# Separate homes for float64 words and float32 results, with loads asked for further ahead

## Chip, cores and metric

The kernel runs on one core of a Trainium2 chip. The time is the device time of one execution in microseconds; three runs of the kernel before are shown, and their median is the time to compare with. A profile is one further execution, recorded by the hardware profiler.

## What is computed

Chunked attention (chunks of 64 positions, head dimension 64, 8 heads, 8 sequences of 576 positions) gives 4608 tokens of 512 features, and two gated products follow:

```python
out  = softmax(q_c @ k_c.T / 8) @ v_c          # per chunk and head
x    = out.transpose(0, 2, 1, 3).reshape(4608, 512)
x    = ((x @ w_a) * (x @ w_b)) @ w_out         # d_ff 1536
y    = (((x @ w1) * (x @ w2)) @ w3) @ w_out2   # d_ff 1024
```

q, k and v are float32. The seven weight matrices come as float64, and the core reads them as pairs of 32-bit words.

## The kernel before

**Blocks.** The tokens are cut into nine blocks of 512. Blocks 0 and 1 are worked plainly, with 12 feature tiles f of 128 columns each (`plain_step`): twelve matmuls for `pa`, twelve for `pb`, a product, and the product with `w_out` summed in four PSUM banks (`acc`). Blocks 2 to 7 go in three pairs with seven products per feature tile (`strassen_step`, tiles `P`); block 8 is worked alone. Then the second gated product does the same with 8 feature tiles. Every float32 operand is held as a high and a low fp32r part, so each product is three matmuls.

**Attention.** It runs beside this in units of one block and two heads, which the text calls U0 to U7 (blocks 0 and 1) and V0 onward (blocks 2 and 3). A unit loads q and k into a tile `qk` and v into a tile `v` (two buffers each, with places of their own for a few of the first units), turns q and k with matmuls (`t`, line 467), makes scores (`s`), softmax on VectorE and ScalarE (`e`), turns the result (`f`, line 480) and multiplies with v (`x`, line 396).

**Converting weights.** Class `Conv` turns one tile of 128 x 512 float64 numbers into float32. `load` (line 167) takes one tile of 3 x 512 words per partition from a slot: 2 x 512 raw words that a DMA of 512 KB fills (line 173), and 512 words `b` for the result. `s1` works on VectorE and ScalarE in place (lines 179, 182, 185), `s2` on VectorE (line 193) leaves the float32 result in `b`. What becomes of it is a sink: a pair tile `w` in high and low parts, stored to DRAM as `dw` and, in float32, as `d32`; a `wo` tile, stored as `dwo`; or a plain float32 copy in DRAM. These stores are put in a list and issued on GpSimd's queue by `tick` (line 151).

**Pump and slots.** `Pump` keeps the 76 conversion jobs in order: 36 in the first two blocks, 24 in the pair of blocks 6 and 7, 16 in block 8. A slot is a tag of the one SBUF pool. In the first part six tags take turns (Y0, Y1, Y2, xo4, xo5, xo6), later three (Y0 to Y2, then xo1, xo2, G2). Since raw words and result share a tile, the next load into a tag has to wait until the store that reads the result has landed. Loads are asked for so that three jobs are loaded and not done in the first part, and two later.

**Order.** The program's order is written by hand. Each engine works through its own list in order. Pieces of attention and conversion are emitted between matmul groups by `Track`, by a running sum of costs. SyncE's queue (SP) carries nearly all loads: q, k, v, the weights, the conversions. An instruction that waits there holds up every load behind it. Each SP load also waits on one of eight semaphores that are given in turn (DMAHW0 to DMAHW7), so it waits until the load eight places ahead has landed.

Of the kernel before, what the change touches and what calls it, by code (L numbers as in the profile page):

```python
# [9 lines left out]
F32 = mybir.dt.float32  # L10
F32R = mybir.dt.float32r
I32 = mybir.dt.int32
# [5 lines left out]
P = 128  # L18
NT = 512
# [59 lines left out]
def chunk_attention_two_gated_products(  # L79
# [23 lines left out]
    nc = tc.nc  # L103
# [6 lines left out]
    NF = [FA // P, FB // P]  # L110
# [7 lines left out]
    pool = ctx.enter_context(tc.tile_pool(name="pool", bufs=1))  # L118
# [27 lines left out]
    def settle(n):  # L146
        while asks["done"] < n and asks["left"]:
            nc.sync.dma_start(*asks["left"].popleft())  # L148
            asks["done"] += 1

    def tick(every=False, loads=0):
        settle(asks["done"] + loads)
        for s in stores:
            s[0] += 1
        while stores and (every or stores[0][0] > 1):
            _, queue, to, src = stores.popleft()
            queue.dma_start(to, src)  # L157


    class Conv:  # L160
# [3 lines left out]
        def __init__(self, src, name, k=1):  # L164
            self.src, self.k, self.nm = src, k, name

        def load(self, slot, queue=None):
            self.out = slot.pop("out", None)
            t = pool.tile([P, 3 * NT], I32, name=f"cv_{self.nm}", **slot)
            self.b = t[:, 2 * NT :]  # L170
            raw = t[:, : 2 * NT]
            to = raw.rearrange("p (k n) -> p k n", k=self.k) if self.k > 1 else raw
            (queue or nc.sync).dma_start(to, self.src)
            r = raw.rearrange("p (n two) -> p n two", two=2)
            self.lo, self.hi = r[:, :, 0], r[:, :, 1]
# [10 lines left out]

        def s2(self):
            b = self.b
            if self.out:
                self.w = pool.tile([P, NT], F32, tag=self.out, name=f"cw_{self.nm}")  # L190
            else:
                self.w = b.bitcast(F32)
            nc.vector.scalar_tensor_tensor(
                self.w.bitcast(I32), self.hi, 3, b, op0=ALU.logical_shift_left, op1=ALU.bitwise_or
            )

    class Pump:
# [4 lines left out]
        def __init__(self):  # L202
            self.jobs, self.done, self.begun, self.loaded = [], 0, 0, 0
            self.cap, self.ahead, self.last = 0, 2, None

        def add(self, jobs):
            self.jobs.extend(jobs)

        def load(self, slot, queue=None):
            if self.loaded < self.cap:  # L210
                self.jobs[self.loaded][0].load(slot, queue)
                self.loaded += 1

        def begin(self, n):
            while self.begun < min(n, self.loaded):
                self.jobs[self.begun][0].s1()
                self.begun += 1
# [13 lines left out]
            self.done += 1  # L231

        def flush(self):
            last, self.last = self.last, None
            if last:
                last[0]()
                last[1]()
# [790 lines left out]
    def attention_begins(units):  # L1028
        for u in units[:2]:
            u.load1()  # L1030
            u.load2()
# [45 lines left out]
    def fuse(i):  # L1077
        t = w3t.pop(i)
        ps = bank("D", f"wf_{i}")
        for jj in range(NF[1]):  # L1080
            for wp, gp in SEQ:
                nc.tensor.matmul(  # L1082
                    ps,
                    t[:, gp, jj],
                    wo2[jj // 2][:, jj % 2, wp],
                    start=(jj == 0 and (wp, gp) == SEQ[0]),
                    stop=(jj == NF[1] - 1 and (wp, gp) == SEQ[-1]),
                )
        w = pool.tile([P, 2, DM], F32R, tag="qk", name=f"wf_{i}", bufs=2)
        split(w[:, 0], w[:, 1], ps, nc.vector)  # L1090
        store(dwo[1][i], w.bitcast(F32))

    with tc.manual_schedule():
# [3 lines left out]
        pump = Pump()  # L1097
# [8 lines left out]
            for m, w in enumerate((w1, w2)):  # L1106
                pump.add([float32_job(col_conv(w, f, f"1_{f}_{m}"), d32[1][f][:, m])])
        pump.cap = 3 * NF[0]
        slots = {"n": 0}

        def slot(kind):
            slots["n"] += 1
            n = slots["n"]
            if kind == "L":
                return dict(tag=["xo1", "xo2", "G2"][n % 3])
            return dict(tag=["Y0", "Y1", "Y2", "xo4", "xo5", "xo6"][n % kind])

        def conv_piece():
            def emit():
                pump.run()  # L1120
                while pump.loaded < min(pump.cap, pump.done + 3):
                    pump.load(slot(6))

            return (2.4, False, emit)

        def later_conv(n, kind):

            pump.ahead = 1

            def load():  # L1130
                if pump.loaded < min(pump.cap, pump.done + 2):
                    pump.load(slot(kind))

            begin = lambda: pump.begin(pump.done + 1)
            one = [(1.1, False, begin), (0.7, False, pump.run), (0.3, False, load)]
            return one * n
# [16 lines left out]

        U = [First(T, hp, T) for T in range(2) for hp in range(NHP)]
        for i in range(3):
            pump.load(slot(6), nc.scalar)
        for u in U[:NHP]:
            u.load1()
            u.load2()
# [14 lines left out]
        for t in range(NHP + 3):  # L1174
            if 2 <= t < NHP + 2:
                U[t - 2].soft2()
            if t >= 3:
                U[t - 3].apply()
                U[t - 3].put()
            if 1 <= t < NHP + 1:  # L1180
                U[t - 1].scores()
            if t < NHP:
                U[t].turn()
            if 2 <= t < NHP + 2:
                U[t - 2].flip()
            if 1 <= t < NHP + 1:
                U[t - 1].soft1()
            if t in (1, 2):
                U[t + 3].load1()
            if t in (3, 4):  # L1190
                U[t + 1].load2()
            if t in (1, 2, 4, 5, 6):
                pump.run()
            if t < 3:
                pump.load(slot(6), nc.scalar)
            tick(loads=8)
        units = unit_list(1)
        both = attention_pieces(U[NHP:] + units)
# [3 lines left out]
        for n, (T, f) in enumerate(order):  # L1202
            if T == 0:
                conv = Track([conv_piece()] * (1 if f == 0 else 3), 5 if f + 1 < AHEAD else 8)
                if f + 1 == NF[0]:
                    conv = None
# [104 lines left out]
        def between(got):  # L1311


            w3s, sums = [], []
            turns = [(i, c) for i in range(NF[1]) for c in range(2)]
            for n_, ic in enumerate(turns + [None] * 2):
                if n_ >= 2 and n_ % 2 == 0:
                    w3s.append((1.5, True, lambda i=n_ // 2 - 1: fuse(i)))
                if ic:
                    w3s.append((1.0, True, lambda ic=ic: turn_w3(*ic)))  # L1320
            su = [Sums(1, f, dict(tag=f"xo{3 + f % 2}")) for f in range(READY)]
            sums += [(0.1, False, su[0].load), (0.1, False, su[1].load)]
            for f in range(READY):
                sums += su[f].early_pieces()
                if f + 2 < READY:
                    sums.append((0.1, False, su[f + 2].load))
            conv = later_conv(2 * NF[1], "L")
            return merged((0, 1, w3s), (0, 1, conv), (0.5, 1, sums), (0, 0.5, x2_pieces([0, 1], got)))

        PTS = 7  # L1330
# [3 lines left out]
        j, places = 0, plain[0]  # L1334
        for ph, sb in [(0, sb) for sb in range(1, NSB + 1)] + [(1, sb) for sb in range(NSB + 1)]:
# [5 lines left out]
            if lone:  # L1341
                x, pieces = lone_pieces(x32, f"{ph}{sb}")
                pieces = pieces + o2_pieces()
                pump.cap = len(pump.jobs)
                slots["n"] = -1
                pieces += [(0.1, False, lambda: pump.load(slot("L")))] * 2
            elif not begins:
                x, pieces = strassen_pieces(x32, f"{ph}{sb}", sb == NSB)
            if ph == 0 and sb == 1:
# [5 lines left out]
                pieces = pieces + first_sums[0].pieces()  # L1355
            steps, at, conv = NF[ph], [], []
            if ph == 0 and not lone:
                units = unit_list(sb + 1)
                attention_begins(units)
                if sb == 1:  # L1360
                    settle(units[0].qk_end)
                    load_part(ph, 1, 3)
                work = attention_pieces(units)
                n_pts = PTS * steps + steps - 4
                if sb == NSB - 1:
                    pump.cap += 3 * NF[1]
                    pump.load(slot(3))
                    pump.load(slot(3))
                    conv = later_conv(3 * NF[1], 3)
                    work = merged((0, 1, work), (0, 1, conv))  # L1370
                    n_pts = PTS * steps
                at.append(Track(work, n_pts - 3))
            if not begins:
                burst(ph, j + 1, places, pieces, [] if conv else at, state.pop("ready", None))
            if lone:
# [16 lines left out]
                class After:  # L1392
                    n = 0
# [19 lines left out]
            j, places = block_steps(ph, sb, x, at)  # L1413
# [51 lines left out]
```

## Time and profile before

| What | Value |
|---|---|
| runs | 1654.66, 1654.49, 1661.31 us, median 1654.66 us |
| profiled execution | 1660.61 us, of which the span from first to last instruction is 1658.8 us |
| TensorE (PE) matmuls busy | 95% of the span |
| VectorE (DVE), ScalarE (ACT), GpSimd (POOL) busy | 51%, 33%, 30% |
| mean granted TensorE clock | 0.984 of full |
| DMA | 400.37 MB, mean 241 GB/s |

Busy shares are means over stages that differ. The first 120 us have a PE that is busy six to eight tenths of the time, and after that nine tenths or more. So the rows to read are single gaps of PE and what ended them, and the rows of the SP queue, on which the loads behind those gaps were issued.

### The profile page before, as it was taken

The numbers are of one execution on the slowest core, as the hardware profiler recorded it, in microseconds if no ns is written. First come the engines' busy times: TensorE is split into PE (matmuls) and PEld (weight loads), VectorE is DVE, ScalarE is ACT, GpSimd is POOL, SyncE is SP. The second block draws the span as 40 slices with busy tenths as digits, with TensorE's granted clock in tenths as the row PEclk, the third lists the DMA queues.
The fourth block names the chain that finished last, engine by engine and source line by source line (L and its number), as shares of the span: only waits on it lengthen the run. The fifth ranks groups of instructions, "written<-read, shape, count | busy, mean of one in ns | idle before, by whom it ended". The sixth has DMA issues, their size and how long they took to land.

```text
span 1658.8 us, 24429 instructions
## 1 busy us (share of the span) xinstructions
PE 1568.2 (95%) x8968; PEld 1256.4 (76%) x8968; DVE 852.7 (51%) x1384; ACT 551.8 (33%) x989; POOL 489.7 (30%) x502
## 2 busy tenths in 40 slices
PE   5789999899999999899999899999999999999998
PEld 4568777677776777677777677788878878878887
DVE  5657755777865455645676234544452352342331
ACT  5544444332242222332234222333332332331322
POOL 1213333222252111432224211223432331331432
PEclk8889999999999999999999999999999999999999
DMA  8768876878777777788986888886776676666684
GB/s 222 225 197 268 254 234 190 255 243 240 229 222 212 213 219 211 214 232 299 321 299 216 295 308 303 311 289 247 249 236 213 218 237 211 223 227 200 219 292 160
DMA packets 289975, 400.37 MB, mean 241 GB/s; under 512 B 175680, under 2 KB 196160, under 8 KB 289856
## 3 DMA queue, kind: packets, MB, share of 16 engines
q1 hardware_dynamic: 262688, 309.67, 61.3%
q0 software_dynamic: 23616, 81.80, 12.8%
q10 hardware_dynamic: 3552, 7.34, 1.2%
q8 instruction: 71, 1.16, 0.3%
q14 instruction: 48, 0.39, 0.1%
HBM read 312.74 MB, written 85.98 MB: 240 GB/s over the span
## 4 chain that ended last, share of the span: by engine, by line
PE 75%; DMA 7%; DVE 6%; issue 4%; ACT 3%; SPq 2%; POOL 2%; POOLq 0%; ACTq 0%; DVEq 0%
PE P L829 38%; PE acc L858 19%; PE pa L815 4%; PE pb L815 4%; PE wf L1082 3%; SPq L148 2%; PE pb0L L815 2%; PE pa0L L815 2%; DMA wo<-dwo 2%; PE x L396 1%; DMA cv_w<-in_moe_w_dram 1%; DVE xP L243 1%; DMA qk<-in_q_dram 1%; DMA cv_o<-in_moe_w_out_dram 1%; DVE c L917 1%
## 5 line engine op out<-in xcount | busy, mean ns | idle before, releaser
L829 PE MATMUL P<-xP,w 128*128 128x512 f32 (+1 forms) x3102 | 715.3, 383 | 19.9 <-DVE c L917 12.5
L829 PEld LDWEIGHTS P<-xP,w 128*128 128x128 f32 x3102 | 557.2, 188 | 147.2 <-DVE c L917 18.0
L917 DVE TENSOR_TENSOR c<-P,c 128x512 f32<-128x512 f32 (+1 forms) x228 | 150.5, 662 | 333.2 <-PE P L829 332.2
L914 ACT COPY c<-P 128x512 f32<-128x512 f32 (+1 forms) x228 | 128.6, 564 | 226.4 <-PE P L829 226.1
L945 POOL TENSOR_TENSOR G<-c,c 128x512 f32<-128x512 f32 x68 | 89.4, 1315 | 337.9 <-DVE c L917 337.8
L242 ACT CAST gh<-c 128x512 fp32r<-128x512 f32 x68 | 42.3, 622 | 329.7 <-DVE c L944 329.7
L243 POOL TENSOR_TENSOR gl<-c,gh 128x512 fp32r<-128x512 f32 x68 | 90.2, 1327 | 177.4 <-ACT gh L242 177.4
L858 PE MATMUL acc<-gh,wo 128*128 128x512 f32 x384 | 139.1, 400 | 0.0
L944 DVE TENSOR_TENSOR c<-P,c 128x512 f32<-128x512 f32 x68 | 47.0, 691 | 136.0 <-PE P L829 136.0
L858 PE MATMUL acc<-wo,gh 128*128 128x512 f32 x320 | 111.2, 391 | 0.5 <-ACT gh L242 0.5
L858 PEld LDWEIGHTS acc<-gh,wo 128*128 128x128 f32 x384 | 72.9, 190 | 16.6
L243 DVE TENSOR_TENSOR xP<-xP,xP 128x512 fp32r<-128x512 f32 (+1 forms) x56 | 64.2, 1187 | 25.3 <-ACT xP L242 25.2
L815 PE MATMUL pa<-xq,w 128*128 128x512 f32 x288 | 76.1, 416 | 0.0
L858 PE MATMUL acc<-gl,wo 128*128 128x512 f32 x192 | 75.6, 394 | 0.0
L157 POOL DMA_DIRECT2D dw<-w x58 | 32.5, 560 | 133.0 <-DVE w L243 79.2
L815 PE MATMUL pb<-xq,w 128*128 128x512 f32 x288 | 71.1, 396 | 0.0
L858 PEld LDWEIGHTS acc<-wo,gh 128*128 128x128 f32 x320 | 60.1, 188 | 13.9 <-ACT gh L242 1.0
L815 PEld LDWEIGHTS pa<-xq,w 128*128 128x128 f32 x288 | 57.1, 201 | 13.1
L867 ACT COPY ev<-acc 128x512 f32<-128x512 f32 x72 | 42.4, 589 | 71.8 <-PE acc L858 67.0
L858 PE MATMUL acc<-wo,gl 128*128 128x512 f32 x160 | 63.0, 394 | 0.8 <-POOL gl L243 0.8
L815 PEld LDWEIGHTS pb<-xq,w 128*128 128x128 f32 x288 | 53.0, 188 | 10.9
L1082 PE MATMUL wf<-wo,w3t 128*128 128x512 f32 x192 | 50.2, 421 | 4.8 <-DVE w3t L243 4.6
(154 smaller groups left out, 2327.2 us busy)
## 6 DMA issues: line engine op xcount, KB each, us to landing
w<-dw SPq DMA_DIRECT2D x213, 512.0 KB, 4.3
wo<-dwo SPq DMA_DIRECT2D x168, 512.0 KB, 4.5
dw<-w POOLq DMA_DIRECT2D x58, 512.0 KB, 4.8
w<-dw SPq DMA_DIRECT2D x87, 256.0 KB, 3.4
d<-cv POOLq DMA_DIRECT2D x40, 256.0 KB, 4.7
su<-d SPq DMA_DIRECT2D x20, 512.0 KB, 5.5
cv_o<-in_moe_w_out_dram SPq DMA_DIRECT2D x18, 512.0 KB, 5.8
x2d<-ev POOLq DMA_DIRECT2D x36, 256.0 KB, 4.8
```

The source lines that it names most:

```text
L148: nc.sync.dma_start(*asks["left"].popleft())
L242: nc.scalar.copy(dst_h, src)
L243: eng_l.tensor_tensor(dst_l, src, dst_h, op=ALU.subtract)
L815: nc.tensor.matmul(ps, w[m][:, kk // 2, wp, kk % 2], xq[kk // 2][:, kk % 2, xp], start=(n == 0), stop=(n == 3 * KM - 1),)
L829: nc.tensor.matmul(ps, w[:, wp, kt], x[:, kt, xp], start=(begins and n == 0), stop=(n == 5), skip_group_check=True,)
L858: nc.tensor.matmul(acc[m], a, b, start=(f == 0 and (wp, gp) == SEQ[0]), stop=(f == NF[ph] - 1 and (wp, gp) == SEQ[-1]),)
L867: nc.scalar.copy(t, acc[m])
L914: nc.scalar.copy(t, src)
L917: add = lambda o, a, b: nc.vector.tensor_tensor(o, a, b, op=ALU.add)
L944: nc.vector.tensor_tensor(g, last, c11, op=ALU.mult)
L945: nc.gpsimd.tensor_tensor(g_place(ph, nm.split("_")[0], f, gplaces), c22, c12, op=ALU.mult)
L1082: nc.tensor.matmul(ps, t[:, gp, jj], wo2[jj // 2][:, jj % 2, wp], start=(jj == 0 and (wp, gp) == SEQ[0]), stop=(jj == NF[1] - 1 and (wp, g ...
```

## The change

Raw words and results get homes of their own. `homes` names tags for raw words and tags for results; a tag of 4 x 512 words holds two raw homes or four result homes. In the first part there are eight of each (raw in Y0, Y1, xo4, xo5; results in Y2, xo6), later four of each. The homes are taken in turn and are not allocated anew. Loads are asked for until five jobs are loaded and not done (before three), later three (before two), and three instead of two loads are put ahead of the work in the later parts. `flush` now calls `tick(True)` first, so that waiting stores are issued before the last job's low part.

```diff
-        def load(self, slot, queue=None):
-            self.out = slot.pop("out", None)
-            t = pool.tile([P, 3 * NT], I32, name=f"cv_{self.nm}", **slot)
-            self.b = t[:, 2 * NT :]
-            raw = t[:, : 2 * NT]
+        def load(self, raw, b, queue=None):
+            self.b = b
...
+        def homes(self, raws, bs):
+            self.raw_tags, self.b_tags = raws, bs
+            self.raws, self.bs, self.n = [], [], 0
+
+        def home(self, places, tags, k, size):
+            per = 4 * NT // size
+            n = k % (per * len(tags))
+            if len(places) <= n:
+                t = pool.tile([P, 4 * NT], I32, tag=tags[n // per], name=f"cv{self.loaded}_{tags[n // per]}")
+                places.extend(t[:, i * size : (i + 1) * size] for i in range(per))
+            return places[n]
...
-        def load(self, slot, queue=None):
+        def load(self, queue=None):
             if self.loaded < self.cap:
-                self.jobs[self.loaded][0].load(slot, queue)
+                raw = self.home(self.raws, self.raw_tags, self.n, 2 * NT)
+                b = self.home(self.bs, self.b_tags, self.n, NT)
+                self.jobs[self.loaded][0].load(raw, b, queue)
                 self.loaded += 1
+                self.n += 1
...
         def flush(self):
+            tick(True)
             last, self.last = self.last, None
...
+        pump.homes(["Y0", "Y1", "xo4", "xo5"], ["Y2", "xo6"])
...
-                while pump.loaded < min(pump.cap, pump.done + 3):
-                    pump.load(slot(6))
+                while pump.loaded < min(pump.cap, pump.done + 5):
+                    pump.load()
...
-                if pump.loaded < min(pump.cap, pump.done + 2):
-                    pump.load(slot(kind))
+                if pump.loaded < min(pump.cap, pump.done + 3):
+                    pump.load()
...
-                slots["n"] = -1
-                pieces += [(0.1, False, lambda: pump.load(slot("L")))] * 2
+                pump.homes(["xo1", "xo2"], ["G2"])
+                pieces += [(0.1, False, lambda: pump.load())] * 3
...
-                    pump.load(slot(3))
-                    pump.load(slot(3))
-                    conv = later_conv(3 * NF[1], 3)
+                    pump.homes(["Y0", "Y1"], ["Y2"])
+                    for _ in range(3):
+                        pump.load()
+                    conv = later_conv(3 * NF[1])
```

The order of instructions on PE, DVE and ACT stays as it was. On POOL the low part of each `wo` tile moves behind two stores. On SP the loads move. First place: the SP queue after block 0's attention loads, where the first conversions of the main loop are asked for. `cv` are conversion loads, `qk1_2` the q and k of unit U6, and behind each row stands what it waits for (DMAHW a landed load, DMASW a landed store). Before:

```order
L173 DMA cv_0_2_0_682<-in_moe_w_a_dram 128x4x256 [waits DMAHW2_49,DMASW1_49,DVE_49]
L173 DMA cv_0_2_1_684<-in_moe_w_b_dram 128x4x256 [waits DMAHW3_49,DMASW3_49,DVE_49]
L173 DMA cv_o2_686<-in_moe_w_out_dram 128x1024 [waits DMAHW4_49,Pool_49]
L148 DMA qk1_2_702<-in_q_dram 16x4x64 [waits DMAHW5_49,PE_49]
L148 DMA qk1_2_702<-in_q_dram 16x4x64 [waits DMAHW6_49]
L148 DMA qk1_2_702<-in_q_dram 112x4x64 [waits DMAHW7_49]
L148 DMA qk1_2_702<-in_q_dram 112x4x64 [waits DMAHW0_49]
L173 DMA cv_0_3_0_829<-in_moe_w_a_dram 128x4x256 [waits DMAHW1_49,DMASW6_49,DVE_49]
L148 DMA qk1_2_702<-in_k_dram 16x4x64 [waits DMAHW2_49]
L148 DMA qk1_2_702<-in_k_dram 16x4x64 [waits DMAHW3_49]
L148 DMA qk1_2_702<-in_k_dram 112x4x64 [waits DMAHW4_49]
L173 DMA cv_0_3_1_888<-in_moe_w_b_dram 128x4x256 [waits DMAHW5_49,DMASW0_49,DVE_49]
```

The same place now:

```order
L170 DMA cv6_xo5_681<-in_moe_w_a_dram 128x4x256 [waits DMAHW2_49]
L170 DMA cv6_xo5_681<-in_moe_w_b_dram 128x4x256 [waits DMAHW3_49]
L170 DMA cv0_Y0_250<-in_moe_w_out_dram 128x1024 [waits DMAHW4_49,DVE_49]
L170 DMA cv0_Y0_250<-in_moe_w_a_dram 128x4x256 [waits DMAHW5_49,DVE_49]
L170 DMA cv2_Y1_254<-in_moe_w_b_dram 128x4x256 [waits DMAHW6_49,DVE_49,Activation_49]
L148 DMA qk1_2_701<-in_q_dram 16x4x64 [waits DMAHW7_49,PE_49]
L148 DMA qk1_2_701<-in_q_dram 16x4x64 [waits DMAHW0_49]
L148 DMA qk1_2_701<-in_q_dram 112x4x64 [waits DMAHW1_49]
L148 DMA qk1_2_701<-in_q_dram 112x4x64 [waits DMAHW2_49]
L170 DMA cv2_Y1_254<-in_moe_w_out_dram 128x1024 [waits DMAHW3_49,DVE_49,Activation_49]
L148 DMA qk1_2_701<-in_k_dram 16x4x64 [waits DMAHW4_49]
L148 DMA qk1_2_701<-in_k_dram 16x4x64 [waits DMAHW5_49]
```

The waits on stores (DMASW) are gone from the conversion loads, five of them stand in a row where three stood, and a sixth stands between q and k.

Second place: SP at the start of the pair of blocks 6 and 7. `wo0_2` and `wo0_3` are the weights of the third and fourth of the `acc` groups that PE works next, `qk8_0` the first unit of block 8. Before:

```order
L715 DMA w0_1_3_7034<-dw0_1_1_69 128x512
L173 DMA cv_o2_0_7049<-in_moe2_w_out_dram 128x1024
L173 DMA cv_o2_1_7051<-in_moe2_w_out_dram 128x1024
L701 DMA wo0_2_7057<-dwo0_2_166 128x1024
L148 DMA qk8_0_7045<-in_q_dram 32x16x32 x4
L148 DMA qk8_0_7045<-in_k_dram 32x16x32 x4
L701 DMA wo0_3_7117<-dwo0_3_167 128x1024
```

The same place now:

```order
L726 DMA w0_1_3_7004<-dw0_1_1_69 128x512
L170 DMA cv36_Y0_7019<-in_moe2_w_out_dram 128x1024 x2
L170 DMA cv38_Y1_7023<-in_moe2_w_out_dram 128x1024
L712 DMA wo0_2_7029<-dwo0_2_166 128x1024
L148 DMA qk8_0_7015<-in_q_dram 32x16x32 x4
L148 DMA qk8_0_7015<-in_k_dram 32x16x32 x4
L712 DMA wo0_3_7089<-dwo0_3_167 128x1024
```

A third conversion load of 512 KB stands ahead of `wo0_2` and `wo0_3`.

Third place: SP in block 8, where the loads `su1_0` and `su1_1` (float32 pairs from which VectorE forms sums) stand behind two conversion loads. Before:

```order
L173 DMA cv_1_4_0_9517<-in_moe2_w1_dram 128x4x256 [waits DMASW1_49,DMAHW3_49,DVE_49,Activation_49]
L1228 DMA x2_1_3_9525<-x2d_1_3_215 128x512 [waits DMAHW4_49]
L173 DMA cv_1_4_1_9561<-in_moe2_w2_dram 128x4x256 [waits DMASW2_49,DMAHW5_49,DVE_49,Activation_49]
L735 DMA su1_0_9563<-d32_1_0_156 128x1024 [waits DMAHW6_49]
L735 DMA su1_1_9565<-d32_1_1_157 128x1024 [waits DMAHW7_49]
```

The same place now:

```order
L170 DMA cv60_xo1_8964<-in_moe2_w2_dram 128x4x256 [waits DMAHW4_49,DVE_49,Activation_49]
L1232 DMA x2_1_3_9469<-x2d_1_3_215 128x512 [waits DMAHW5_49]
L170 DMA cv62_xo2_8968<-in_moe2_w1_dram 128x4x256 [waits DMAHW6_49,DVE_49,Activation_49]
L746 DMA su1_0_9506<-d32_1_0_156 128x1024 [waits DMAHW7_49,DMASW5_49,DMASW4_49]
L746 DMA su1_1_9508<-d32_1_1_157 128x1024 [waits DMAHW0_49,DMASW7_49,DMASW6_49]
```

The conversion loads wait for no store any more; the `su` loads now name the stores that wrote what they read.

## Rows read from the trace of the kernel before

**Rows 1.** The page: busy us (share), instructions by engine; ScalarE's evictions (mean ns, idle)

```profile
PE 1568.2 (95%) x8968; PEld 1256.4 (76%) x8968; DVE 852.7 (51%) x1384; ACT 551.8 (33%) x989; POOL 489.7 (30%) x502
...
L914 ACT COPY c<-P 128x512 f32<-128x512 f32 (+1 forms) x228 | 128.6, 564 | 226.4 <-PE P L829 226.1
```

**Rows 2.** Stretches: PE, PEld, DVE, ACT, POOL busy, clock, DMA share, GB/s

```profile
50.00:55.00 5.00, 2.34 (x44) 1.90 (x41) 1.75 (x4) 3.08 (x4) 0.62 (x1) 0.88 1.06 307
80.00:100.00 20.00, 12.67 (x141) 9.20 (x141) 8.88 (x18) 8.15 (x13) 4.26 (x7) 0.87 0.86 255
```

**Rows 3.** SP's waits, first 300 us: us in total, times, longest

```profile
SPq L173 <- DMA d<-cv: 59.4, 15, 13.0
```

**Rows 4.** SP's timeline near 60 us: start, us, instruction

```profile
50.73 3.75 SPq L148 DMA_DIRECT2D qk<-in_k_dram  x3
63.68 0.37 SPq L173 DMA_DIRECT2D cv<-in_moe_w_b_dram  x1
64.09 0.59 SPq L148 DMA_DIRECT2D qk<-in_k_dram  x1
```

**Rows 5.** PE's timeline, 60 to 112 us: start, us, instruction [idle before <-releaser]

```profile
68.19 1.09 PE L467 MATMUL t<-ident,qk 128*128 128x128 f32 x4 [4.32 <-DMA qk<-in_k_dram]
...
70.53 1.12 PE L480 MATMUL f<-ident,e 128*128 128x128 f32 x4
...
81.86 0.63 PE L467 MATMUL t<-ident,qk 128*128 128x128 f32 x4 [1.91 <-DMA qk<-in_k_dram]
...
94.80 1.09 PE L467 MATMUL t<-ident,qk 128*128 128x128 f32 x4 [2.21 <-DMA qk<-in_k_dram]
97.09 1.12 PE L480 MATMUL f<-ident,e 128*128 128x128 f32 x4 [1.20 <-ACT kT L468]
...
99.94 5.36 PE L815 MATMUL pa<-xq,w 128*128 128x512 f32 x12
...
108.61 3.03 PE L815 MATMUL pa<-xq,w 128*128 128x512 f32 x12
```

**Rows 6.** DVE's timeline: the softmax results of U5 and U7

```profile
67.90 0.69 DVE L370 TENSOR_TENSOR e<-e,sm 128x512 f32<-128x512 f32 x1
...
94.12 0.69 DVE L370 TENSOR_TENSOR e<-e,sm 128x512 f32<-128x512 f32 x1
```

**Rows 7.** All conversion loads of the tile cv: issue to landing

```profile
DMA to landing us min/median/max: 2.8/4.7/9.5
```

**Rows 8.** DVE's timeline, 740 to 800 us: conversions that waited for their load

```profile
741.85 0.43 DVE L179 TENSOR_SCALAR cv_o<-cv_o 128x512 int32<-128x512 uint32 x1 [3.06 <-DMA cv_o<-in_moe_w_out_dram]
...
751.71 0.43 DVE L179 TENSOR_SCALAR cv_o<-cv_o 128x512 int32<-128x512 uint32 x1 [5.47 <-DMA cv_o<-in_moe_w_out_dram]
...
798.56 0.43 DVE L179 TENSOR_SCALAR cv_w<-cv_w 128x512 int32<-128x512 uint32 x1 [4.57 <-DMA cv_w<-in_moe_w_dram]
```

**Rows 9.** PE's timeline, 700 to 803 us: its long gaps

```profile
700.57 0.47 PE L858 MATMUL acc<-gh_5b,wo 128*128 128x512 f32 x1 [3.48 <-DMA wo<-dwo]
...
744.22 4.46 PE L829 MATMUL P<-xP,w 128*128 128x512 f32 x18 [2.08 <-ACT c L914]
...
754.12 2.93 PE L829 MATMUL P<-xP,w 128*128 128x512 f32 x6 [3.36 <-DVE c L917]
...
800.37 2.81 PE L829 MATMUL P<-xP,w 128*128 128x512 f32 x11 [1.58 <-DVE c L944]
```

**Rows 10.** SP's timeline, block 8

```profile
990.17 0.49 SPq L1228 DMA_DIRECT2D x<-x2d  x1
997.39 0.38 SPq L173 DMA_DIRECT2D cv<-in_moe_w_dram  x1
997.82 0.98 SPq L735 DMA_DIRECT2D su<-d  x2
```

**Rows 11.** DVE's timeline, block 8

```profile
1004.37 0.43 DVE L743 TENSOR_TENSOR su<-su 128x256 f32<-128x256 f32 x1 [2.61 <-DMA su<-d]
```

**Rows 12.** PE's timeline, block 8

```profile
990.57 5.79 PE L1082 MATMUL wf<-wo,w3t 128*128 128x512 f32 x24
...
1008.50 7.38 PE L1082 MATMUL wf<-wo,w3t 128*128 128x512 f32 x24 [2.23 <-DVE w3t L243]
```

More of the change, by code (lines that the diff above doesn't have):

```diff
@@ L188, in s2 @@
             b = self.b
[L189 to L192, printed above, removed]
+            self.w = b.bitcast(F32)
             nc.vector.scalar_tensor_tensor(
@@ L204, in __init__ @@
             self.cap, self.ahead, self.last = 0, 2, None
+            self.raws, self.bs, self.n = [], [], 0
+        def homes(self, raws, bs):
+            self.raw_tags, self.b_tags = raws, bs
+            self.raws, self.bs, self.n = [], [], 0
+        def home(self, places, tags, k, size):
[5 more added lines that the diff above has]
+            return places[n]
         def add(self, jobs):
             self.jobs.extend(jobs)
-        def load(self, slot, queue=None):
+        def load(self, queue=None):
             if self.loaded < self.cap:
-                self.jobs[self.loaded][0].load(slot, queue)
+                raw = self.home(self.raws, self.raw_tags, self.n, 2 * NT)
+                b = self.home(self.bs, self.b_tags, self.n, NT)
+                self.jobs[self.loaded][0].load(raw, b, queue)
                 self.loaded += 1
+                self.n += 1
         def begin(self, n):
@@ L1120, in emit, with later_conv @@
                 pump.run()
-                while pump.loaded < min(pump.cap, pump.done + 3):
-                    pump.load(slot(6))
+                while pump.loaded < min(pump.cap, pump.done + 5):
+                    pump.load()
             return (2.4, False, emit)
-        def later_conv(n, kind):
+        def later_conv(n):
             pump.ahead = 1
             def load():
-                if pump.loaded < min(pump.cap, pump.done + 2):
-                    pump.load(slot(kind))
+                if pump.loaded < min(pump.cap, pump.done + 3):
+                    pump.load()
             begin = lambda: pump.begin(pump.done + 1)
@@ L1155, in chunk_attention_two_gated_products @@
         for i in range(3):
-            pump.load(slot(6), nc.scalar)
+            pump.load(nc.scalar)
         for u in U[:NHP]:
@@ L1194, in chunk_attention_two_gated_products @@
             if t < 3:
-                pump.load(slot(6), nc.scalar)
+                pump.load(nc.scalar)
             tick(loads=8)
@@ L1326, in between @@
                     sums.append((0.1, False, su[f + 2].load))
-            conv = later_conv(2 * NF[1], "L")
+            conv = later_conv(2 * NF[1])
             return merged((0, 1, w3s), (0, 1, conv), (0.5, 1, sums), (0, 0.5, x2_pieces([0, 1], got)))
```

7 lines of the change are left out of this document (removed).

## The prediction

> **What bounds the kernel now.** I read the page's busy shares first: TensorE (PE) is busy 95% of the span [rows 1], so the change can pay only where PE stands idle or runs at the lower clock. The stretches show where: from 80 to 100 us PE is busy 12.67 of 20 us at a mean clock of 0.87 [rows 2]. Then SP's waits: in the first 300 us its queue stood 59.4 us at the conversion loads of line 173, fifteen times, until a store of an earlier result had landed [rows 3]. The timeline of SP shows who pays. Three of the four k loads of unit U6 were out at 54.48 (50.73 + 3.75), then a conversion load stood until 63.68, and the fourth k load went out at 64.09 [rows 4]. PE waited 4.32 us for it, and 1.91 and 2.21 us for the k of U7 and V0, whose loads stood in the same queue [rows 5]. The reader should see one pattern three times: a load that PE needs behind a load that waits for a store.
>
> From about 105 us on PE is nearly full until the later conversions. There VectorE (DVE) itself waits for conversion loads, and PE gaps follow at once; and in block 8 SP stands again. These are terms 2 and 3.
>
> **Term 1, blocks 0 and 1.** The DMASW waits go from the conversion loads, so SP no longer stands there. The raw home they take was read by VectorE eight jobs before. I follow PE's chain. U6's k in time takes away 4.32 us, but the next link, U5's `f`, needs the softmax result that DVE ends at 67.90 + 0.69 = 68.59 [rows 6], and nothing in that DVE work waits for a load. `f` ran at 70.53 [rows 5], so 1.9 us are gained and DVE is late next. U7's k: 1.91 more, together 3.8. V0's k: 2.21 more, 6.0. U7's `f`, at 97.09, needs `e`, ended at 94.81 [rows 6]; moved by 3.8 that is 91.0, and 97.09 - 6.0 = 91.1, so the 6.0 hold. The `pa` behind it took 5.36 us at the lower of the clock's two levels (1.2 GHz), against 3.03 for the next one at 2.4 [rows 5]: if PE does not run dry before it, 2.3 us more. The gap before it shrinks but does not vanish, so I count half, 1.2.
>
> Against this stands traffic. From 50 to 55 us the DMA engines were full (share 1.06, 307 GB/s [rows 2]). Two more conversion loads of 512 KB now stand ahead of U6's k, which is 1.05 MB / 307 GB/s = 3.4 us. So the last k goes out at about 54.5 + 0.6 + 3.4 = 58.5 and lands 4.7 to 9.5 us later (median and longest of such loads [rows 7]), at 63.2 to 68.0; `f` of U5 loses nothing while k lands before about 67. U7 and V0 have less slack, and I take 2.2 off for them. Term 1: 6.0 + 1.2 - 2.2 = 5.0 saved, with bounds at 8.3 (no lateness, full clock) and at a loss of 15 (rival D).
>
> The Trainium skill (DMA: Bandwidth & Descriptors, "Queues, rings and completion order") says that a DMA engine takes a queue's descriptors in ring order, which speaks against long loads ahead of short ones. The spread from 2.8 to 9.5 us [rows 7] agrees with it, though no row separates the order from the load. By that rule alone, five loads ahead of U6's q put it off by an estimated 2.6 MB at 307 GB/s, 8.5 us, and the slack above would be nearly used up; the 2.2 us stand for that here.
>
> **Term 2, blocks 6 and 7.** Three conversions waited for their load, 3.06, 5.47 and 4.57 us [rows 8], and PE gaps of 2.08, 3.36 and 1.58 us start right there [rows 9]: DVE and ScalarE hold PSUM evictions behind the waiting conversion. Each load now stands one job earlier, and the first of the three goes out before the stretch. A job takes several us here, so the waits of DVE should go. I count 1.5 of the first gap (an eviction by ScalarE, 564 ns [rows 1], is late next) and the other two whole: 6.4. Behind the 3.36 us gap six matmuls took 2.93 us where eighteen had taken 4.46 (six: 1.5), so 1.4 for the clock, 7.8 in all. What it costs: a third load ahead of `wo0_3`, for which PE already waited 3.48 us at 700.57 [rows 9]: 0.52 MB / 307 GB/s = 1.7 us longer, and half of another 1.4 us for a clock that may fall in that gap. Net 5.4 saved; bounds 8.4 saved and 3.1 lost.
>
> **Term 3, block 8.** SP stood from 990.66 to 997.39 at a conversion load, and the `su` loads behind it went out at 997.82 [rows 10]. DVE waited 2.61 us for them [rows 11], PE 2.23, and the 24 matmuls after the gap took 7.38 us against 5.79 in an earlier group [rows 12]. With up to 6.7 us in hand the wait goes: 2.23 + 1.6 = 3.8 saved. The bounds are 3.8 and nothing; I take the upper, since 6.7 is far more than 2.61.
>
> **The rest I cost at nothing.** The wait for a store now stands on DVE (line 179 of the changed kernel), before it writes a result home. Behind it in DVE's list stand PSUM evictions that PE needs. But it is the store of eight jobs ago, later four, and each store is issued by the next job or two; if that cover fails, each such wait is a PE gap like the three of term 2. On POOL a `wo` low part goes behind two store issues, and is not needed before a later step. The other SP waits in the first part lie beside a busy PE.
>
> Sum: 5.0 + 5.4 + 3.8 = 14.2 us, 1660.61 - 14.2 = 1646.4 on the profiled execution. That execution lies 5.95 us over the median of 1654.66. If this excess sits in the stalls that go, 1646.4 is the answer against the median also; if not, it is 1640.5. I take the middle, 1643.
>
> **Rivals.**
>
> B: the DMA is the bound at the start. q and k come late as before, behind more conversion loads, and term 1 is nil; the full engines at 50 to 55 us speak for it, the 63.2 to 68.0 us against it. 1643 + 5 = 1648.
>
> C: other engines take over in blocks 6 to 8. PE then waits for evictions or `w3t` instead of conversions, and terms 2 and 3 give nothing. For: in two of the three places it is an eviction that PE names. Against: these follow the DVE wait within 1.5 us. 1643 + 5.4 + 3.8 = 1652.
>
> D, slower: eight loads in flight. Each SP load waits for the load eight places ahead to land, so at the median 4.7 us a load costs 0.59 us of queue, as much as its issue (0.59 [rows 4]). If landings rise, the queue slows by an eighth of the rise per load. From U6's first k to V0's last k stand about 35 loads. At a mean of 4.7 + 8 x 6.0 / 35 = 6.1 us the gain of 6.0 is gone; at the longest landing, 9.5 us [rows 7], it is 35 x 4.8 / 8 = 21 us, a loss of 15. The same would hold up blocks 6 and 7, so term 2 goes too: 1643 + 5 + 15 + 5.4 = 1668. For it: 1.06 of DMA share. Against: from 80 to 100 us the share is 0.86, and only two loads are added once, not at each job.
>
> E: the change doesn't do what it says. SP stands as long as before, at the q and k buffers or the v buffers instead of the stores, which come free only as PE goes on. Then 1654.7.
>
> **How the numbers follow.** Forecast 0.60 (1636 to 1649), B 0.15, C 0.11, D 0.07, E 0.07. What a measurement of this kernel can tell from no change is about 0.5%, 8 us: below 1646.4 is faster, above 1662.9 slower. The forecast gives 0.54 of its 0.60 to faster, B 0.06 and C 0.02: 0.62 faster; D 0.07 slower; 0.31 the same. A range from 1635 to 1654 holds the forecast, B and C, and leaves out D and E with most of the rest, under 2 in 10.
>
> **What would show it.** Right: no wait of SP at the conversion loads for stores; the gaps of PE before U7's and V0's `t` gone or under 0.5 us, and `f` of U5 waiting for DVE's `e` instead; the three DVE waits of blocks 6 and 7 and the one for `su` gone; the gap before `wo0_3` longer by 1 to 2 us. Wrong: landings of q and k beyond 6 us in the first 100 us; DVE waits at the result homes; PE gaps in blocks 6 to 8 of the same sum under other names.

## The result, and the profile after

| | before | changed |
|---|---|---|
| runs, median (lowest to highest) | 1654.86 (1654.49 to 1661.31) us | 1638.49 (1637.16 to 1640.50) us |
| profiled execution, span | 1660.61, 1658.8 us | 1640.50, 1638.7 us |

The ratio is 0.9889, with a 95% interval of 0.9868 to 0.9910: 1.1% faster. Forecast were 1643 us, range 1635 to 1654.

**Blocks 0 and 1.** SP's waits in the first 300 us of the changed kernel (total us, times, longest) answer to [rows 3]; behind them PE's own wait for the softmax result, over the whole span:

```profile
SPq L148 <- PE x L407: 51.6, 9, 13.1
...
SPq L170 <- DVE cv_xo L187: 2.4, 3, 1.9
```

```profile
PE f L491 <- DVE e L381: 12.2, 7, 3.2
```

The wait for stores is gone. SP stands nearly as long as before, but at v loads whose buffers PE has yet to free. No q or k that PE needs is held up behind them: SP's timeline and PE's show it. SP's timeline, against [rows 4]:

```profile
52.04 1.72 SPq L170 DMA_DIRECT2D cv_Y<-in_moe_w_out_dram  x1
53.81 4.41 SPq L148 DMA_DIRECT2D qk<-in_k_dram  x3
58.49 0.38 SPq L170 DMA_DIRECT2D cv_xo<-in_moe_w_a_dram  x1
58.98 0.58 SPq L148 DMA_DIRECT2D qk<-in_k_dram  x1
```

U6's last k goes out at 58.98 (58.5 was forecast, 64.09 before) and lands 6.5 us later, at 65.48. PE's timeline, against [rows 5], and then DVE's softmax results of U5 and U7, against [rows 6]:

```profile
65.68 0.63 PE L478 MATMUL t<-ident,qk 128*128 128x128 f32 x4 [1.12 <-DVE cv_Y L179]
...
69.44 1.09 PE L491 MATMUL f<-ident,e 128*128 128x128 f32 x4 [2.44 <-DVE e L381]
...
78.16 1.04 PE L478 MATMUL t<-ident,qk 128*128 128x128 f32 x8
...
88.65 1.06 PE L478 MATMUL t<-ident,qk 128*128 128x128 f32 x8 [0.26 <-PE acc L869]
...
91.63 0.63 PE L491 MATMUL f<-ident,e 128*128 128x128 f32 x4 [1.92 <-DVE e L381]
...
94.00 5.31 PE L826 MATMUL pa<-xq,w 128*128 128x512 f32 x12
...
102.63 3.03 PE L826 MATMUL pa<-xq,w 128*128 128x512 f32 x12
```

```profile
68.60 0.69 DVE L381 TENSOR_TENSOR e<-e,sm 128x512 f32<-128x512 f32 x1
...
90.80 0.69 DVE L381 TENSOR_TENSOR e<-e,sm 128x512 f32<-128x512 f32 x1
```

The `t` of U7 and V0 wait for nothing that matters, and what is late next is `e`: 68.60 + 0.69 = 69.29, and `f` starts at 69.44. The 1.12 us before U6's second `t` at 65.68 are put down to VectorE, but the last k landed only 0.2 us before it. `f` would have waited for `e` all the same. The `pa` behind U7's `f` still takes 5.31 us where the next takes 3.03. The DMA engines stay full near 50 us, and the clock of the stretch from 80 us is no better than in [rows 2], though PE is busy 16.00 of its 20 us there instead of 12.67:

```profile
50.00:55.00 5.00, 2.01 (x22) 1.59 (x26) 2.32 (x6) 3.08 (x4) 2.22 (x3) 0.96 1.11 361
80.00:100.00 20.00, 16.00 (x149) 12.04 (x148) 10.93 (x21) 8.49 (x16) 3.15 (x4) 0.83 0.77 216
```

**Blocks 6 and 7.** Of the three DVE waits of [rows 8] one of 0.77 us is left (745.53). PE's timeline, against [rows 9]:

```profile
692.94 0.76 PE L869 MATMUL acc<-gh_5b,wo 128*128 128x512 f32 x1 [4.42 <-DMA wo<-dwo]
...
749.43 3.06 PE L840 MATMUL P<-xP,w 128*128 128x512 f32 x12 [0.53 <-ACT c L925]
...
752.91 1.67 PE L840 MATMUL P<-xP,w 128*128 128x512 f32 x6 [0.42 <-ACT c L925]
```

The gap at `wo` grew from 3.48 to 4.42 us, and the matmul behind it now takes 0.76 us instead of 0.47: the lower level of the clock. Two further traces of before have gaps of 4.27 and 3.39 us there, both followed by that lower level (their lines stand with those traces below), so most of this difference is one between executions. Instead of 2.08, 3.36 and 1.58 us, PE loses 0.53 and 0.42, to ScalarE's evictions.

**Block 8.** SP's timeline, against [rows 10]; DVE's start on `su`, against [rows 11]; PE's group at the place of the gap, against [rows 12]:

```profile
974.94 0.41 SPq L170 DMA_DIRECT2D cv_xo<-in_moe_w_dram  x1
975.45 1.14 SPq L746 DMA_DIRECT2D su<-d  x2
```

```profile
986.07 0.41 DVE L754 TENSOR_TENSOR su<-su 128x256 f32<-128x256 f32 x1
```

```profile
990.67 5.85 PE L1093 MATMUL wf<-wo,w3t 128*128 128x512 f32 x24
```

No wait is left there; 24 matmuls take 5.85 us instead of 7.38. The `su` loads went out that much earlier but also landed more slowly, 9.6 and 10.4 us after their issue instead of 6.5 and 7.3.

**The ledger.** Both kernels issue the same 8,968 matmuls in the same order. So the start of each can be set against its twin, and the growth of the difference tells in which stretch (times of before) the 20.13 us from trace to trace were gained:

| stretch, us | gained | forecast |
|---|---|---|
| 0 to 500 (term 1) | 6.2 | 5.0 |
| 500 to 530 | 2.5 | 0 |
| 530 to 690 | 0.3 | 0 |
| 690 to 730 (the gap at `wo`) | -3.4 | -2.4 |
| 730 to 810 (term 2) | 8.7 | 7.8 |
| 810 to 990 | 1.2 | 0 |
| 990 to 1030 (term 3) | 3.8 | 3.8 |
| 1030 to the end | 0.8 | 0 |

### The profile page after: what moved, and what is told of

It reads as the page before. It is cut to its first block, busy times and chain, and to the rows that moved or that the text cites. A ratio compares the mean times of both kernels' runs of the same rounds, so it can differ in the third digit from the quotient of the medians.

```text
span 1638.7 us, 24412 instructions
## 1 busy us (share of the span) xinstructions
PE 1561.4 (95%) x8968; PEld 1253.9 (77%) x8968; DVE 854.8 (52%) x1384; ACT 550.5 (34%) x989; POOL 489.9 (30%) x502
## 4 chain that ended last, share of the span: by engine, by line
PE 77%; DVE 7%; DMA 5%; issue 4%; ACT 3%; POOL 2%; SPq 1%; POOLq 0%; DVEq 0%; ACTq 0%
PE P L840 40%; PE acc L869 19%; PE pa L826 4%; PE pb L826 4%; PE wf L1093 3%; DMA wo<-dwo 3%; PE pb0L L826 2%; PE pa0L L826 2%; PE x L407 1%; SPq L148 1%; DVE xP L254 1%; DMA qk<-in_q_dram 1%; DVE c L928 1%; PE s L356 1%; ACT xP L253 1%
## 5 line engine op out<-in xcount | busy, mean ns | idle before, releaser
L869 PEld LDWEIGHTS acc<-wo,gh 128*128 128x128 f32 x320 | 60.1, 188 | 13.4 <-ACT gh L253 1.0
L373 ACT ACTIVATE e<-e 128x512 f32<-128x512 f32 x36 | 22.8, 633 | 94.2 <-DVE e L367 94.2
```

The source lines that it names most:

```text
L869: nc.tensor.matmul(acc[m], a, b, start=(f == 0 and (wp, gp) == SEQ[0]), stop=(f == NF[ph] - 1 and (wp, gp) == SEQ[-1]),)
```

## The experiments

Ratios are to runs of before on the same chip. The theory: in the first part it is the homes apart that gain, because SP no longer stands for stores; in blocks 6 and 7 it is the third load ahead. The rival: depth is what counts everywhere.

**Three ahead in the first part, homes apart.**

```diff
-                while pump.loaded < min(pump.cap, pump.done + 5):
+                while pump.loaded < min(pump.cap, pump.done + 3):
```

> The changed kernel with its separate homes, but in blocks 0 and 1 loads asked for three jobs ahead again instead of five. Theory S (the early gain comes from SP no longer standing at conversion loads for stores, the depth gives nothing there): TensorE is ahead of the kernel before by 6 us at its 112th us as in the changed kernel, time 1638.5 within 1.5 us. Rival A (the early gain comes from loads asked for further ahead): the 6 us go back, 1644 to 1645.

Measured: 1639.16 us, ratio 0.9899 (0.9877 to 0.9920). Five ahead gives nothing over three. In its trace PE stands at U6's `t` no more, and all of the lateness has become a wait for DVE, about as long as the 1.12 and 2.44 us of the changed kernel together:

```profile
68.91 1.08 PE L491 MATMUL f<-ident,e 128*128 128x128 f32 x4 [3.74 <-DVE e L381]
```

**Five ahead, joint slots.** The kernel before, with only this:

```diff
-                while pump.loaded < min(pump.cap, pump.done + 3):
+                while pump.loaded < min(pump.cap, pump.done + 5):
```

> The kernel before with its joint slots, but loads in blocks 0 and 1 asked for five jobs ahead. Theory S: a load now takes the slot of a job finished two jobs ago, whose store has only just been issued, so SP stands longer at the conversion loads than the 59 us before, q and k come later: 1656 to 1662, slower than 1654.9. Rival A: the depth is what counts, 5 to 6 us are gained, 1649.

Measured: 1720.59 us, ratio 1.0392 (1.0365 to 1.0419). The direction was expected, the size was missed by about 60 us. SP's wait in the first 300 us, then PE's longest gaps:

```profile
SPq L173 <- DMA d<-cv: 135.5, 18, 22.4
```

```profile
77.41 1.08 PE L467 MATMUL t<-ident,qk 128*128 128x128 f32 x4 [7.47 <-DMA qk<-in_k_dram]
101.03 1.09 PE L467 MATMUL t<-ident,qk 128*128 128x128 f32 x4 [13.75 <-DMA qk<-in_q_dram]
...
124.25 1.08 PE L467 MATMUL t<-ident,qk 128*128 128x128 f32 x4 [8.48 <-DMA qk<-in_q_dram]
...
156.59 2.15 PE L467 MATMUL t<-ident,qk 128*128 128x128 f32 x8 [13.54 <-DMA qk<-in_q_dram]
```

With six slots, a load five ahead takes the slot of the last but one finished job, whose store has only just been handed on; three ahead it was a job two places older. Eighteen loads waited for a store, 7.5 us in the mean, where fifteen had waited 4.0 us, and the q and k behind them waited as well. The same depth that is free with homes apart costs 3.9% without. This kernel also lacks the `tick(True)` in `flush`.

**Two ahead from block 6 on, homes apart.**

```diff
-                if pump.loaded < min(pump.cap, pump.done + 3):
+                if pump.loaded < min(pump.cap, pump.done + 2):
```

(and two loads in advance instead of three)

> The changed kernel, but in blocks 6 to 8 loads asked for two jobs ahead again and two instead of three ahead of the work. Theory S with depth as the cause of the gain in blocks 6 and 7: VectorE waits again 3 to 5 us at two or three conversions there and TensorE has its gaps of 2 to 3.4 us back, about 10 us lost, while the 3.2 us that the third load ahead of the wo loads cost come back: 1645. The gap at the su loads of block 8 stays away, since SP waits for no store. Rival: in blocks 6 and 7 too it was SP's wait for stores; then nothing is lost there, the 3.2 us come back, 1635.

Measured: 1646.49 us, ratio 0.9948 (0.9925 to 0.9971). The three DVE waits are back, and PE's gaps with them:

```profile
736.04 0.43 DVE L176 TENSOR_SCALAR cv_Y<-cv_Y 128x512 int32<-128x512 uint32 x1 [2.07 <-DMA cv_Y<-in_moe_w_out_dram]
...
746.57 0.43 DVE L176 TENSOR_SCALAR cv_Y<-cv_Y 128x512 int32<-128x512 uint32 x1 [6.15 <-DMA cv_Y<-in_moe_w_out_dram]
...
794.58 0.43 DVE L176 TENSOR_SCALAR cv_Y<-cv_Y 128x512 int32<-128x512 uint32 x1 [4.43 <-DMA cv_Y<-in_moe_w_dram]
```

```profile
738.41 4.41 PE L840 MATMUL P<-xP,w 128*128 128x512 f32 x18 [1.04 <-ACT c L925]
...
748.98 2.93 PE L840 MATMUL P<-xP,w 128*128 128x512 f32 x6 [4.12 <-DVE c L928]
```

So homes apart alone, with two loads ahead, give blocks 6 and 7 nothing, and the third load gives all of term 2; a third load with joint slots was not run. Block 8 kept its gain. The 3.2 us expected back at `wo` did not come: PE's gap there is 3.39 us, again with the lower clock, and in the ledger below that stretch is about 1 us better than in the changed kernel.

**Without the stores issued at `flush`.**

```diff
         def flush(self):
-            tick(True)
```

> The changed kernel without the new tick(True) in flush, so GpSimd's queue has the low part of each wo tile ahead of the two stores again. Theory S: no load waits for these stores any more, so nothing changes: 1638.5 within 1.5 us. Rival: the earlier stores have a part in the gain, and 2 us or more are lost.

Measured: 1639.33 us, ratio 0.9900 (0.9878 to 0.9922): nothing, as expected, as long as homes are apart. With joint slots it is another matter, as the first part put back will show.

**The three loads of blocks 6 and 7 in the burst.** The burst is the pieces of work with which a pair of blocks begins; the loads go to its end, behind the q and k loads and the first `wo` loads.

```diff
-                    for _ in range(3):
-                        pump.load()
+                    pieces += [(0.1, False, lambda: pump.load())] * 3
```

> The changed kernel, with the three conversion loads of blocks 6 and 7 asked for at the end of block 6's first burst instead of ahead of its q, k and wo loads. My theory (the loads ahead of wo cost what term 2 takes off): the gap of PE before the matmul that waits for wo, 4.42 us in the changed kernel, falls to about 1.5 to 2.5 us, the low clock behind it goes, DVE's conversions still find their data, and the time is 1635 (1633 to 1637). Rival 1: the gap is that of the q and k loads, which stand ahead of the wo load in SP's queue as well; it stays at 3.5 us or more and the time at 1638. Rival 2: the first conversions of blocks 6 and 7 now wait for their loads, and a gap of 2 us or more stands between 725 and 770 us: 1640 or more.

Measured: 1635.55 us, ratio 0.9867 (0.9847 to 0.9887). The gap, then the stretch from 680 us in the changed kernel and in this one (the number before the last two is the granted clock):

```profile
687.84 0.47 PE L869 MATMUL acc<-gh_5b,wo 128*128 128x512 f32 x1 [1.65 <-DMA wo<-dwo]
```

```profile
680.00:720.00 40.00, 33.78 (x136) 26.02 (x135) 22.11 (x23) 15.86 (x29) 16.97 (x15) 0.96 0.86 250
```

```profile
680.00:720.00 40.00, 35.87 (x151) 27.59 (x150) 21.88 (x22) 18.14 (x33) 18.32 (x17) 1.00 0.90 283
```

The gap is 1.65 us and the clock stays up. The loads ahead of `wo` were its cause, and both rivals fall. This moves all three loads, two of which stood ahead of `wo` in the kernel before too.

**The same, with three ahead in the first part** (the first and the last edit together).

> The kernel before this one (loads of blocks 6 and 7 in the burst), and three loads ahead instead of five in the first part. My theory: five ahead gave nothing over three, so this is the same time, 1635 (1633 to 1637), and PE's gap in front of U6's t shorter by about 1 us. Rival: with the later cost gone, the lead of five in the first part shows, and this is slower by 2 us or more.

Measured: 1637.62 us, just above the range, ratio 0.9877 (0.9855 to 0.9899), no different from the one before. PE's gap in front of U6's `t`, 1.29 us there, is gone, but the wait of `f` for `e` grew from 2.25 to 3.75 us.

**The later part alone, and the first part alone.** In the first kernel the first part has six joint slots and three ahead again, in the second the later parts have three joint slots and two ahead. Both keep the `tick(True)` in `flush`. Of the edits, the line that joins the first part's slots:

```diff
-        pump.homes(["Y0", "Y1", "xo4", "xo5"], ["Y2", "xo6"])
+        pump.homes(["Y0", "Y1", "Y2", "xo4", "xo5", "xo6"], [])
```

> The changed kernel with the first part put back: six joint slots and three loads ahead there, homes apart and three ahead from block 6 on. My theory: the two parts add up. SP's wait for stores in the first 300 us is back at about 59 us, with PE's gaps of 4.3, 1.9 and 2.2 us before the t of U6, U7 and V0; the rest of the gain stays: 1645 (1643 to 1648). Rival: a time gained early runs into a later bound, so the early part is worth nothing by the end: 1639.

> The changed kernel with the later parts put back: three joint slots, two loads ahead, two loads in advance from block 6 on; the first part as changed. My theory: term 1 alone is left, 6 us: 1649 (1647 to 1651), and the gap of 2.2 us at w3t in block 8 is back, since there it is the homes apart and not the depth that gained (with homes apart and two ahead it was gone, and the time 1646.5). Rival: the gain in block 8 came from somewhere else in the changed order, the gap doesn't come back, and the time is 1646.5.

Measured: 1641.63 us, ratio 0.9915 (0.9891 to 0.9938), and 1646.71 us, ratio 0.9936 (0.9915 to 0.9957). Both expectations were too slow: the halves gain 0.85% and 0.64%, the whole 1.1%, so they add up only at the edge of their intervals. For the first part alone it is the rival's time and the rival's sign that came. Two things stand out. With the first part put back, SP waited 44.0 us at the conversion loads and not 59.4:

```profile
SPq L170 <- DMA d<-cv_Y: 24.4, 6, 7.4
SPq L170 <- DMA d<-cv_xo: 19.6, 7, 4.2
```

PE's gaps before the `t` of U6, U7 and V0 were 1.23, 1.62 and 0.26 us, not the 4.3, 1.9 and 2.2 expected. The kernel gives a cause: with `tick(True)` in `flush`, GpSimd issues the store behind which U6's fourth k load stands ahead of the `wo` low part. That store in the kernel before, the same in this one, and the conversion load that waited for it (63.68 in [rows 4]):

```profile
58.40 0.55 POOL L157 DMA_DIRECT2D d<-cv  x1
```

```profile
51.27 0.55 POOL L157 DMA_DIRECT2D d<-cv_xo  x1
58.67 0.37 SPq L170 DMA_DIRECT2D cv_xo<-in_moe_w_b_dram  x1
```

It goes out 7 us earlier and lands at 58.6 instead of 63.6. So this kernel is not the first part as it was, and part of term 1 may be there with joint slots: up to 3.6 us by the ledger below, where the third trace of before has 1.9 without the early stores. That is one reason why the halves gain more than the whole. No run has the early stores alone.

And with the later parts put back, the gap in block 8 did not return, though SP stood 4.6 us there (979.91 + 0.50 to 985.01):

```profile
979.47 0.38 SPq L170 DMA_DIRECT2D cv_G<-in_moe_w_dram  x1
979.91 0.50 SPq L1237 DMA_DIRECT2D x<-x2d  x1
985.01 0.38 SPq L170 DMA_DIRECT2D cv_xo<-in_moe_w_dram  x1
985.43 0.98 SPq L751 DMA_DIRECT2D su<-d  x2
```

```profile
990.71 0.43 DVE L759 TENSOR_TENSOR su<-su 128x256 f32<-128x256 f32 x1
```

Here the store goes out no earlier than before: in both kernels GpSimd issues it 15.6 us before PE is done with the matmuls ahead of that place (1006.27 - 990.68 and 995.25 - 979.67). So either the first trace of before was an unlucky one, or the homes are not the cause in block 8. The next two runs ask for it; the expectation takes the earlier landing in the first part for chance as well.

**The kernel before, a second and a third trace.** No edit.

> The kernel before, unchanged, for a second trace of it. With the first part put back and the same order of SP, the store that U6's fourth k load stands behind landed 5 us earlier than in the first trace of before. My theory: the landing of a store differs from execution to execution, and the first trace is a late one; here the load goes out at 58 to 62 us instead of 64.09, PE's gap before U6's t is 1 to 3 us instead of 4.32, block 8's gap at w3t is under 1 us, and the span is 1650 to 1656. Rival: the traces of one kernel agree, the gaps are 4.3 and 2.2 us again, and the difference lies in the kernels.

> The kernel before, unchanged, for a third trace. Theory and rival as for the second: by the theory the span and PE's early gaps go together (a trace that is longer has the larger sum of gaps before 110 us and in block 8).

Measured: 1660.91 and 1660.59 us, spans 1659.1 and 1658.8. PE's first gap, the one at `wo` in block 6 and the one in block 8, second trace, then third (here with the `f` behind the first gap):

```profile
68.02 1.09 PE L467 MATMUL t<-ident,qk 128*128 128x128 f32 x4 [4.29 <-DMA qk<-in_k_dram]
...
699.21 0.77 PE L858 MATMUL acc<-gh_5b,wo 128*128 128x512 f32 x1 [4.27 <-DMA wo<-dwo]
...
1008.89 6.47 PE L1082 MATMUL wf<-wo,w3t 128*128 128x512 f32 x20 [2.09 <-DVE w3t L243]
```

```profile
66.27 0.63 PE L467 MATMUL t<-ident,qk 128*128 128x128 f32 x4 [1.45 <-DMA qk<-in_k_dram]
...
69.69 0.68 PE L480 MATMUL f<-ident,e 128*128 128x128 f32 x4 [2.10 <-DVE e L370]
...
699.36 0.77 PE L858 MATMUL acc<-gh_5b,wo 128*128 128x512 f32 x1 [3.39 <-DMA wo<-dwo]
...
1008.52 6.70 PE L1082 MATMUL wf<-wo,w3t 128*128 128x512 f32 x21 [1.96 <-DVE w3t L243]
```

The theory half falls. The early gap does differ from execution to execution (4.32, 4.29, 1.45 us), but the span does not follow it, and the gap in block 8 is there each time (2.23, 2.09, 1.96). The kernel with five ahead and joint slots has it too (2.09). In the kernel with the first part alone, the first `su` load landed 5.3 us after its issue (985.43) against 6.5 (997.82), and SP went on 5.3 us after GpSimd issued the store that it waited for (979.67 to 985.01) against 6.7 (990.68 to 997.39). Together that is the 2.6 us of [rows 11]. From the store's issue to the landing of `su` it took 11.0 us here, and 13.4 to 13.7 us in the four traces with the gap. No run shows what made them quicker.

**The changed kernel and the one with its loads in the burst, on one chip.**

> The changed kernel, unchanged, on the same chip as the one with its loads in the burst. Ratio to before 0.989 (0.987 to 0.991), and a gap before the matmul that waits for wo in block 6 of 4 us or more, since it came in four traces of kernels with three loads ahead of wo.

> The kernel with the three loads in the burst, a second time, against the changed kernel on one chip. My theory: 3 us below it (1 to 5), from the gap at wo (1.7 us instead of 4.4) and the low clock behind it. Rival: no difference, the two ratios of before came from different chips.

Measured: 1638.86 us, ratio 0.9888 (0.9867 to 0.9908), with a gap of 3.65 us at `wo`, somewhat under the 4 expected; and 1636.47 us, ratio 0.9880 (0.9858 to 0.9903), with its longest gap there 1.10 us. The second is 2.4 us lower, and all three measurements with the loads in the burst (0.9867, 0.9877, 0.9880) lie below the four with homes apart throughout, a third load and the loads in front (0.9888 to 0.9900). The intervals overlap, so about 2 us is likely and not shown. Its traces do show 2.9 us in that stretch (below).

**All traces in one ledger.** Gained against the mean of the three traces of before, by the starts of the matmuls as above, us:

| kernel | 0 to 112 | 500 to 530 | 690 to 730 | 730 to 810 | 990 to 1030 |
|---|---|---|---|---|---|
| before, three traces | -1.0, -0.9, 1.9 | -0.9, 1.7, -0.8 | 1.6, -1.3, -0.3 | 0.9, -1.1, 0.3 | -0.1, 0.0, 0.1 |
| changed, two traces | 5.0, 7.5 | 1.6, 1.7 | -1.8, -1.5 | 9.6, 9.8 | 3.7, 3.6 |
| three ahead; no stores at `flush` | 7.4, 4.7 | 2.0, 1.5 | -0.6, -0.8 | 9.9, 10.6 | 3.6, 3.7 |
| loads in the burst, three traces | 8.0, 4.6, 5.9 | 2.2, 2.4, 2.1 | 1.7, 2.3, 1.0 | 10.5, 10.6, 10.5 | 3.7, 3.6, 3.7 |
| two ahead later | 7.2 | -2.7 | -0.6 | 0.1 | 3.7 |
| first part alone | 6.3 | 1.6 | 0.7 | 2.2 | 3.7 |
| later part alone | 3.6 | 1.6 | -1.1 | 9.5 | 3.6 |
| joint slots, five ahead | -46.8 | 1.4 | 1.2 | 2.0 | 0.0 |

The 2.9 us: 1.7 (mean of 1.7, 2.3, 1.0) against -1.2 (mean of -1.8, -1.5, -0.6, -0.8). In this stretch the traces line up by the loads ahead of `wo`: none, 1.0 to 2.3; two, -1.3 to 1.6; three, -1.8 to -0.6.

## Why the prediction was right

**Term 1, the mechanism right, two parts of the sum wrong.** Every step of the chain is in the trace: U6's last k at 58.98, `f` of U5 waiting for `e`, `t` of U7 and V0 without a wait, U7's `e` ending at 91.49 (91.0 forecast). The first link gave 1.1 us (`f` at 69.44 for 70.53) and not 1.9, since U5's `e` itself ended 0.7 later; by the `pa` behind U7's `f` nearly all of the 6.0 was there (94.00 for 99.94). So the 2.2 us taken off for lateness were hardly due: the loads did land later (in the first 110 us a median of 5.0 to 5.5 us for the two conversion tiles against 4.9, longest 10.1 against 6.5; U6's four q loads 8.1 to 10.2 against 5.7 to 6.7), but what was left in hand covered it. The 1.2 us for the clock did not come: a gap of 1.92 us stood before `f`, and `pa` behind it took 5.31 us. That the two errors nearly cancel, 6.2 for 5.0, is luck. In the third trace of before U6's `t` waits only 1.45 us, and `f` then waits 2.10 us for `e`: that `e` is late next holds without the change too, and part of this term belongs to the one execution from which it was read. That SP's wait for stores was the cost is shown. Which part of the change is needed to take it away is not: homes apart suffice without the deeper loading and, in another run, without the early stores, but the early stores took part of it with joint slots, and homes apart also make eight raw homes out of six slots. More joint slots were not run.

**Term 2, the mechanism right, the gain too small and the loss too large.** 8.7 for 7.8 was gained in the stretch (9.5 to 10.6 against the mean of the three traces of before), since the first gap (2.08 us) went whole where ScalarE's eviction was to be late next. At `wo` 3.4 for 2.4 was lost between the two first traces, but the first trace of before is the best of its three there. Against their mean the five traces with three loads in front lose 0.6 to 1.8 us, and the half of a clock loss in the forecast isn't shown as a cost of the change: two of three traces of before run at the lower level there too. The kernel with its loads in the burst shows that loads in front of `wo` make that gap, and the one with two ahead shows that the gain needs the third load.

**Term 3, the size right, the cause shown with one exception.** With homes apart and two ahead the gap was gone, so depth isn't needed. In all four traces of kernels with joint slots and the old `flush`, SP stood 5.0 to 6.7 us and the gap is there. In the one of the first part alone SP stood 4.6 us and it is not, by the 2.6 us that store and `su` loads landed sooner. So the stand made the gap only together with landings as slow as in those four. The upper bound was the lucky choice: of the 6.7 us in hand the slower landing of `su` took 3.

**What wasn't forecast** is 2.5 us at 512 to 521: PE has a gap at `wo` there in all kernels (1.96 us before, 1.50 after), and from 516 to 525 us the granted clock is 0.81 in two of the three traces of before, and 1.00 in the third and in both of the changed kernel. The trace of before whose clock stayed up has the changed kernel's time there (1.7 in the ledger), and the kernel with two ahead later lost 2.7 there with a clock of 0.57 from 508 to 516 us. So it goes with the clock's level, which no step explains. The other 2.3 us are shifts that no run was made for.

**From the trace to the median.** The sum of 14.2 was 20.1 from trace to trace and 16.4 from median to median. I took half of the 5.95 us by which the profiled execution lay above the median as lying in the stalls that go. The two further traces of before lie as high (1660.91, 1660.59), but runs without the profiler beside them have a median of 1658.04 and reach 1662.80. So whether the excess belongs to profiled executions or to chance stays open, and that the middle came near is luck in part.

**The rivals.** B fell: U7's and V0's q and k came in time, and U6's last k before `e` was done. C fell: the other engines took 0.95 us in blocks 6 and 7. D's landings rose by under 1 us in the median, short of the 6.1 us where it decides. E was half right, which the forecast had at 0.07: SP does stand nearly as long as before, at the v buffers (51.6 us for 59.4), but no gap of PE from 60 to 112 us names a v load.

**The signs.** One sign of being wrong came and proved a poor one: landings of q and k beyond 6 us in the first 100 us. U6's q took up to 10.2 us, but the kernel before already had 6.7, and the gain came all the same. The other two did not: DVE waits for no store at the result homes, and the gaps in blocks 6 and 7 did not come back under other names.

## What to carry over

Where a buffer takes a load and also holds a result until its store has landed, the load queue waits for stores; give raw data and results buffers of their own before asking for more loads ahead, for with joint slots two more ahead cost 3.9%, and apart they were free. Where buffers stay joint, look at when the store is issued: 7 us earlier on GpSimd's queue was 5 us earlier for the load that waited. What a waiting load costs isn't the length of the wait (59.4 and 51.6 us here) but which loads stand behind it and whether their consumer is busy. Ask for the early loads of a new stretch behind the loads that the running stretch needs.

## What was not expected of the hardware

The clock behind a gap of PE at `wo` doesn't follow from the gap's length alone: in traces of the kernel before, the granted clock was 0.81 in the mean from 516 to 525 us, behind gaps of 1.96 and 2.14 us, and 1.00 from 700 to 710 us behind one of 3.48 us. At that same place the third trace had a gap of 3.39 us, and the matmul behind it took 0.77 us, at the lower level, instead of 0.47. And single landings differ from execution to execution enough to make a gap of 4.3 us one of 1.45 in the same kernel, while the span of the three traces stayed within 0.3 us.
